# Block 0's output rows stored from the GpSimd queue behind batch 3's loads instead of from SyncE

## The chip, the cores and the metric

The kernel runs on one core of one Trainium2 chip. The metric is the device time of one execution in microseconds (us), the median over runs. A core has five engines that each work through a queue of their own in order: TensorE (PE, matrix products; PEld are its weight loads), VectorE (DVE), ScalarE (ACT), GpSimd (POOL) and SyncE (SP). They wait for each other through semaphores, and DMA queues move data between DRAM and the on-chip memory.

## What is computed

Eight batches of eight heads with 576 tokens of 64 values go through a linear attention with a norm per head, and the result, seen as 4608 tokens of 512 values, through a bilinear feed-forward layer of width 1536:

```python
def _attn_ref(q, k, v, g_norm):
    kv = np.einsum('bhsd,bhse->bhde', k, v)
    out = np.einsum('bhsd,bhde->bhse', q, kv)
    rms = np.sqrt(np.mean(out * out, axis=-1, keepdims=True) + 1e-06)
    return (out / rms * g_norm).astype(np.float32)

def _moe_ref(x, w_a, w_b, w_out):          # x: 4608 x 512
    a = x @ w_a
    b = x @ w_b
    return (a * b @ w_out).astype(np.float32)
```

Inputs and output are float32; inside, bfloat16 and float16 are used.

## The kernel before

The tokens are cut into nine blocks of 512. Block 0 is computed in the plain way: `std_block` forms a and b, and `o_std` (lines 951 to 986) multiplies by the output weights for four tiles of 128 tokens (L964), copies each result out of its accumulator bank into the buffer `o_sb` (ACT, L980), and stores it to DRAM (line 985, through `store`, line 920; the DMA itself is L932). Blocks 1 to 8 use a scheme with seven products in place of eight: `wino_block` (L860 products, L420 copies on ACT, L879 sums on DVE, L914 elementwise product a*b) and `o_block`/`o_unit` for the output product (L1029 products, L1061 copies on ACT, L1067 sums on DVE, L1014 operand sums on DVE). In `wino_block` four products of a unit go through one accumulator bank X, one after the other: p1, p6, p7, p4. Between two of them ACT copies the bank out (e1, e2, e3 into `u`), and after p4 it copies the bank into `c` (c21) and so frees it for the next unit's p1.

Batches 0 and 1 are loaded by pieces at the start. Batches 2 to 7 are loaded one at a time by `load_node` (line 671) from the POOL queue: two DMAs of q into a DRAM scratch `scr` (L682), five of k (L688, L689) and two of v (L694, L698). SP then transposes the scratch into `qT` (L703). Before the next batch's loads stands a one-element copy on POOL (L677, `gate_t`) that waits until the `qT` of the batch before has landed; for batch 7 a second one (L679) waits also for the normed tokens of batch 5. When k and v are there, PE forms kv (L645, 20 matmuls; the last four of them use the data of L698), ACT copies it (L660, L661), and PE multiplies by q (L353). Batches 5 to 7 take another way, `token_tiles`: five token tiles a batch (L560 on PE, L575 on ACT, L579 on DVE, L586 on ACT, L593 on DVE into `xt`), stored to DRAM by SP (L600), read back transposed by SP (four L615 into `xp`), and scaled by ACT (four L621).

The order on each engine is not written out by hand. Each piece of work is a node with an engine, an assumed duration, a due time and its dependencies, and `Plan.order()` (line 104) lists them: at each step it takes the node that can start first on its engine by the assumed times, with the due time to break ties. What a reader of a node's result has to wait in addition stands in `LAT` (line 74) by the producing engine, 0.1 us where an engine is not listed. For kv of a batch the plan assumes that its data is there `kv_us` after the load node (line 708). These numbers decide the order alone; on the chip the semaphores decide the times. In `load_node` the due times come from the batch's window (`at_win`).

DMAs of one kind of queue take eight completion semaphores in turn. A DMA issued from POOL therefore waits until the POOL DMA eight before it has landed.

Of the kernel before, what the change touches and what calls it, by code (L numbers as in the profile page):

```python
# [70 lines left out]


class Plan:
    LAT = {"PE": 0.27, "SP": 2.2, "ACT": 0.2, "DVE": 0.18}
    OWN = {"ACT": 0.12, "DVE": 0.13}

    def __init__(self, t0):
# [12 lines left out]
    @classmethod  # L90
    def after(cls, n, lat=None):
        return n.end + (cls.LAT.get(n.eng, 0.1) if lat is None else lat)

# [44 lines left out]
def kernel(  # L138
# [11 lines left out]
    nc = tc.nc  # L150
# [162 lines left out]
    def xcols(p, t0, n):  # L313
        return xp[p // 2][:, p % 2, t0 % R : t0 % R + n]
# [91 lines left out]
    def mm_us(n, cols):  # L406
        return n * (cols / 2400 + 0.0025)

    def act_us(n, bias=False):
        return (0.155 if bias else 0.06) + n / 1200  # L410
# [260 lines left out]
    def load_node(b, prio, dep, xt=None):  # L671
        ld = {"k": Buf(RK), "v": Buf(RV), "q": Buf(RQT)}
        scr = scr_pool.tile([NP, S, 2, D], BF16, name="scr", tag="scr")

        def issue():
            if dep is not None:
                nc.gpsimd.tensor_copy(gate_t, dep["q"].tile[0:1, 0, 0:1])  # L677
            if xt is not None:
                nc.gpsimd.tensor_copy(gate_t, xcols(NP - 1, (b - 2) * S, 1)[0:1])  # L679
            qv = q[b].rearrange("(p hl) s d -> hl s p d", hl=2)  # L680
            for hl in range(2):
                nc.gpsimd.dma_start(  # L682
                    out=scr[:, :, hl, :].rearrange("p s d -> s p d"), in_=qv[hl]
                )
            kt = ld["k"].tile
            ks = k[b, :, 0:SA, :].rearrange("h (sp c) d -> sp h c d", c=NCH)
            for c in range(NCH):
                nc.gpsimd.dma_start(out=kt[:, c], in_=ks[:, :, c, :])  # L688
            nc.gpsimd.dma_start(out=kt[0:SB, NCH], in_=k[b, :, SA:S, :].rearrange("h sp d -> sp h d"))  # L689
            for n, src in (("v", v),):  # L690
                t = ld[n].tile[:, 0 : H * (NCH + 1) * D].rearrange(
                    "p (h c d) -> p h c d", h=H, d=D
                )
                nc.gpsimd.dma_start(  # L694
                    out=t[:, :, 0:NCH, :],
                    in_=src[b, :, 0:SA, :].rearrange("h (sp c) d -> sp h c d", c=NCH),
                )
                nc.gpsimd.dma_start(  # L698
                    out=t[0:SB, :, NCH, :], in_=src[b, :, SA:S, :].rearrange("h sp d -> sp h d")
                )  # L700

        def transpose():
            nc.sync.dma_start_transpose(  # L703
                out=ld["q"].tile[:].rearrange("p a s -> p (a s)"),
                in_=scr[:].rearrange("a s h d -> (a s) (h d)"),
            )

        issue_us, q_us, ld["kv_us"] = (15.4, 4.3, 13.0) if dep is None else (9.0, 5.0 if b == 3 else 1.8, 16.0 if b == 3 else 13.0)

        ld["n"] = plan.add(  # L710
            "POOL", issue_us, prio, issue, ([(dep["qn"], 8.0)] if dep else []) + ([(xt, TURN)] if xt else []), [ld["k"], ld["v"]]
        )
        ld["qn"] = plan.add(
            "SP", 2.5, prio, transpose, [(ld["n"], q_us)], [ld["q"]]
        )
        return ld
# [203 lines left out]
    def store(g0, o_sb, queue=None, es=slice(0, d_model)):  # L920
        queue = queue or nc.sync
        i = 0
        while i < 128:
            b, j = divmod(g0 + i, S)
            if b < NE:
                c, sp = divmod(j, EP)
                n = min(128 - i, EP - sp)
                r0, st = b * S + EC * sp + c, EC
            else:
                n = min(128 - i, S - j)  # L930
                r0, st = b * S + j, 1
            queue.dma_start(out=out[r0 : r0 + st * (n - 1) + 1 : st, es], in_=o_sb[i : i + n, es])  # L932
            i += n
# [17 lines left out]
    def o_std(ab, muls, win):  # L951
        w0, w1 = win
        ob = Buf(ROS)
        ng, copied = N0 // 128, []
        for g in range(ng):
            pr = w0 + (w1 - w0) * g / ng
            ps = Buf((RO, RY)[g % 2])

            n1 = None
            for f0 in range(0, FC, OP):  # L960

                def mm(g=g, ps=ps, f0=f0):
                    for fc in range(f0, f0 + OP):
                        nc.tensor.matmul(  # L964
                            ps.tile[:],
                            lhsT=ab.tile[:, fc, g * 128 : (g + 1) * 128],
                            rhs=wo_t[:, fc, :],
                            start=(fc == 0),
                            stop=(fc == FC - 1),
                        )  # L970

                n1 = plan.add(
                    "PE", mm_us(OP, d_model), pr + 0.01 * f0, mm,
                    [(wo_n, 5.8 if f0 + OP <= FC // 2 else 10.6), n1] + [muls[fc] for fc in range(f0, f0 + OP)],
                    [ps] if f0 == 0 else [], [ab],
                )
            o_reads.append(n1)
            n2 = plan.add(
                "ACT", act_us(d_model), pr,
                lambda g=g, ps=ps: nc.scalar.copy(ob.tile[:, g], ps.tile[:]),  # L980
                [n1] + copied[-1:], [ob] if g == 0 else [], [ps],
            )
            copied.append(n2)
            plan.add(
                "SP", 0.45, pr + 1, lambda g=g: store(g * 128, ob.tile[:, g]), [n2], (), [ob]
            )

    def o_unit(r0, ab, muls, osum, pr, du, chunks, pieces, m, w, first, second, X, Y, Z, ob, s2, s3, s4, W):
# [164 lines left out]
    for b in range(2, B):  # L1153
        t = b * S / N0
        at_win[b] = (max(53.0, st[int(t) - 1] + (t % 1) * L[int(t) - 1] - 18), st[int(t)] - 22 + (t % 1) * 12)
        if b >= TB:
            at_win[b] = tuple(x - AHEAD for x in at_win[b])
    loads = {2: load_node(2, 22.5, None)}
    wo_n = load_wo(loads[2])
    turned = {}  # L1160
# [13 lines left out]
    for bi in range(1, nb + 1):  # L1174
        o_win = (st[bi] + 1.0, st[bi + 1] - 1.0) if bi < nb else (st[bi] + O_A, st[bi + 1] + O_B)
        if bi == 1:
            o_std(ab, muls, (o_win[0] + 4.0, o_win[1] + 4.0))
            osum = out_sums(st[2] - 10)
        else:
            o_block(bi - 1, ab, muls, osum, o_win, 2, (RO, RY5, RY5) if B5 <= bi < B6 else (RO, RY, RY), 1)  # L1180
        for b in needs[bi]:
            if b > 2:
                loads[b] = load_node(b, at_win[b - 1][0], loads[b - 1], turned.get(b - 2))
            turned[b] = late_batch(b, loads[b], at_win[b])
        ab, muls = wino_block(bi, (st[bi], st[bi + 1]), wsum)
# [40 lines left out]
```

## Time and profile before

| | us |
|---|---|
| median of 3 runs (295.05 to 295.81) | 295.31 |
| the profiled execution | 295.81 |
| its span, first to last instruction | 293.7 |
| DVE, ACT, POOL busy in the span | 241.4, 191.3, 77.7 |
| L860 matmuls, mean of one (x288 each group) | 0.273 |
| L879 sums on DVE, mean of one (x144) | 0.687 |
| L420 copies on ACT, mean of one (x144) | 0.591 |
| stores of `o_sb` from SP, 256, 192, 128, 64 KB: median to landing | 2.7, 5.2, 2.4, 3.9 |
| loads of v, 512 KB, from POOL: median to landing | 10.7 |

The profiled execution is the slowest of the three runs shown. Times within the span are counted from its first instruction. Matmuls are pipelined: one of 256 columns is listed with 0.27 us, but the next one starts 0.109 us later (two rows of two matmuls start 0.22 us apart), so PE's work is counted in starts, not in listed durations. In the same way DVE's sums of 0.69 us start 0.60 apart, and ACT's copies of 0.59 us 0.47 to 0.50 apart.

### The profile page before, as it was taken

The page shows a single profiled execution, that of the slowest core. Times are in us where ns is not written, and L with a number is a line of the kernel's source. Part 1 is how long each engine was busy: PE and PEld are TensorE (multiplying, and loading weights), DVE is VectorE, ACT ScalarE, POOL GpSimd, SP SyncE. Part 2 cuts the span into 40 slices and gives each one's busy share as a digit, 9 for nine tenths or more (in the row PEclk, how much of TensorE's full clock was granted, in tenths as well). Part 3 has the DMA queues.
Part 4 walks back from the last instruction along what each step waited for, and adds up shares of the span by engine and source line. Part 5 has one row for each costly group of instructions (what it writes and reads, how often), then busy time and mean ns, then how long its engine had stood idle before and what let it go on. Part 6 is the DMA issues. An engine that isn't in the chain of part 4 may idle for free.

```text
span 293.7 us, 6760 instructions
## 1 busy us (share of the span) xinstructions
PE 286.7 (98%) x2646; PEld 237.5 (81%) x2648; DVE 241.4 (82%) x443; ACT 191.3 (65%) x395; POOL 77.7 (26%) x96
## 2 busy tenths in 40 slices
PE   6999999999999999999999999999999999999995
PEld 3645558965888888899988998888988888888884
DVE  5454889893987988799989999979989968698964
ACT  3766767866578777867757866686859546665411
POOL 8844830850092390380000910000000000000000
PEclk9999999999999999999999999999999999999999
DMA  8999999699999999699916999440138000300044
GB/s 177 198 198 199 198 159 167 97 169 181 193 132 169 145 168 171 60 135 204 184 29 132 154 163 156 86 164 20 39 80 173 3 0 2 143 2 0 3 143 143
DMA packets 112644, 36.26 MB, mean 123 GB/s; under 512 B 89061, under 2 KB 108517, under 8 KB 112613
## 3 DMA queue, kind: packets, MB, share of 16 engines
q0 software_dynamic: 77552, 18.44, 66.5%
q1 hardware_dynamic: 34448, 16.70, 27.4%
q10 hardware_dynamic: 612, 0.71, 0.8%
q8 instruction: 20, 0.33, 0.5%
q14 instruction: 12, 0.09, 0.1%
HBM read 37.75 MB, written 14.75 MB: 179 GB/s over the span
## 4 chain that ended last, share of the span: by engine, by line
PE 77%; DVE 9%; DMA 5%; issue 2%; POOL 2%; ACT 2%; SPq 1%; DVEq 0%; ACTq 0%; POOLq 0%
PE bk L860 40%; PE bk L1029 21%; PE bk L387 7%; PE bk L964 3%; DVE c L879 3%; DMA wb_t<-in_moe_w_b_dram 3%; PE bk L645 2%; PE bk L353 1%; PE bk L367 1%; SPq L615 1%; DMA xs<-xt 1%; POOL as L242 1%; DVE xt L593 1%; ACT xp L621 1%; DMA xp<-xs 1%
## 5 line engine op out<-in xcount | busy, mean ns | idle before, releaser
L879 DVE TENSOR_TENSOR c<-bk,u 128x512 f16<-128x512 f32 x144 | 96.5, 687 | 19.7 <-PE bk L860 11.8
L420 ACT COPY u<-bk 128x512 f32<-128x512 f32 x144 | 81.5, 591 | 36.4 <-PE bk L860 29.8
L860 PE MATMUL bk<-xp,wa_t 128*128 128x256 f16 x288 | 55.0, 273 | 0.4 <-ACT c L420 0.3
L860 PE MATMUL bk<-xp,wb_t 128*128 128x256 f16 x288 | 55.0, 273 | 0.0
L860 PEld LDWEIGHTS <-wa_t 128*128 128x128 f16 x384 | 37.1, 98 | 6.1 <-issue 0.8
L1029 PEld LDWEIGHTS <-abt 128*128 128x128 f16 x384 | 37.5, 98 | 4.6 <-issue 0.3
L860 PEld LDWEIGHTS <-wb_t 128*128 128x128 f16 x384 | 37.6, 98 | 4.4
L1029 PE MATMUL bk<-wo_t,abt 128*128 128x256 f16 x288 | 37.0, 273 | 0.1
L860 PE MATMUL bk<-T,sb 128*128 128x256 f16 x192 | 36.6, 273 | 0.0
L860 PE MATMUL bk<-T,sa 128*128 128x256 f16 x192 | 36.6, 272 | 0.0
L420 ACT CAST c<-bk 128x512 f16<-128x512 f32 x48 | 28.0, 587 | 12.1 <-PE bk L860 11.5
L914 DVE TENSOR_TENSOR abt<-c 128x1024 f16<-128x1024 f16 x48 | 32.8, 687 | 0.9
L860 PEld LDWEIGHTS <-sa 128*128 128x128 f16 x288 | 27.9, 98 | 3.6
L860 PEld LDWEIGHTS <-sb 128*128 128x128 f16 x288 | 28.2, 98 | 3.3
L1029 PEld LDWEIGHTS <-as 128*128 128x128 f16 x288 | 28.1, 98 | 3.3
L376 DVE SCALAR_TENSOR_TENSOR xp<-bk,g_col,rs 128x288 f16<-128x288 f32 x40 | 20.3, 514 | 11.2 <-ACT rs L371 11.2
L1061 ACT COPY o_sb<-bk 128x512 f32<-128x512 f32 x30 | 17.6, 586 | 17.3 <-PE bk L1029 16.8
L1029 PE MATMUL bk<-so,as 128*128 128x256 f16 x192 | 25.2, 273 | 0.0
L371 ACT ACTIVATE rs<-bk,eps_t 128x288 f32<-128x288 f32 x40 | 20.1, 507 | 6.4 <-PE bk L367 6.2
L688 POOL DMA_DIRECT2D k_t<-in_k_dram x24 | 21.2, 898 | 0.7 <-issue 0.4
L682 POOL DMA_DIRECT2D scr<-in_q_dram x12 | 19.6, 1636 | 2.4 <-issue 1.2
L1067 DVE TENSOR_TENSOR o_sb<-bk,o_sb 128x512 f32<-128x512 f32 (+1 forms) x26 | 16.7, 647 | 3.4 <-PE bk L1029 2.5
(108 smaller groups left out, 427.7 us busy)
## 6 DMA issues: line engine op xcount, KB each, us to landing
out_dram<-o_sb SPq DMA_DIRECT2D x20, 256.0 KB, 2.7
scr<-in_q_dram POOLq DMA_DIRECT2D x12, 288.0 KB, 7.5
k_t<-in_k_dram POOLq DMA_DIRECT2D x24, 128.0 KB, 7.7
v_t<-in_v_dram POOLq DMA_DIRECT2D x6, 512.0 KB, 10.7
out_dram<-o_sb SPq DMA_DIRECT2D x18, 128.0 KB, 2.4
wa_t<-in_moe_w_a_dram POOLq DMA_DIRECT2D x6, 256.0 KB, 10.7
wb_t<-in_moe_w_b_dram POOLq DMA_DIRECT2D x6, 256.0 KB, 10.9
wo_t<-in_moe_w_out_dram POOLq DMA_DIRECT2D x2, 768.0 KB, 9.5
```

The lines of the kernel that those rows point to most:

```text
L371: nc.scalar.activation(rs, self.s_ps[p, h][:, 0:HF], AF.Abs_reciprocal_sqrt, bias=eps_t)
L376: nc.vector.scalar_tensor_tensor(out=xcols(p, self.b * S + h * HF, HF), in0=self.x_ps[p, h][:, 0:HF], scalar=g_col, in1=self.rs[p, h], op0 ...
L387: nc.tensor.matmul(ps[:, 0:n], lhsT=w[:, kc, fc * 128 : (fc + 1) * 128], rhs=xcols(kc, 0, n), start=(kc == 0), stop=(kc == KC - 1),)
L420: ("ACT", act_us(n), lambda: nc.scalar.copy(*args())),
L682: nc.gpsimd.dma_start(out=scr[:, :, hl, :].rearrange("p s d -> s p d"), in_=qv[hl])
L688: nc.gpsimd.dma_start(out=kt[:, c], in_=ks[:, :, c, :])
L860: nc.tensor.matmul(ps.tile[:, i * n : (i + 1) * n], lhsT=lhs(w, sm)[:, kc, :], rhs=rhs()[:, kc, :], start=start and i == 0 and kc == 0, st ...
L879: lambda: nc.vector.tensor_add(cs(fi, h), full(ps), u.tile),
L914: nc.vector.tensor_mul(t, c[:, :, :, 0], c[:, :, :, 1])
L1029: nc.tensor.matmul(ps.tile[:, sub * EH : (sub + 1) * EH], lhsT=lhs(slice(j, j + 1))[:, 0, sub * 128 : (sub + 1) * 128], rhs=rhs[:, j, :], ...
L1061: lambda: nc.scalar.copy(o(fi, h), bank(X, every)), [dep], takes, frees,
L1067: nc.vector.tensor_add(o(fi, h, subs), bank(ps, subs), other)
```

## The change

In `o_std` the four stores of block 0's output (each two DMAs, since the token rows of batches 0 and 1 cross a boundary: 256 KB a tile, 1 MB together) are issued by POOL and not by SP, with an assumed 1.2 us a node in place of 0.45. `LAT` gets an entry of 6.0 us for POOL, which says when the plan may give `o_sb` to the next writer. And `kv_us` of batch 3 goes from 16 to 14.

```diff
-    LAT = {"PE": 0.27, "SP": 2.2, "ACT": 0.2, "DVE": 0.18}
+    LAT = {"PE": 0.27, "SP": 2.2, "ACT": 0.2, "DVE": 0.18, "POOL": 6.0}
...
-        issue_us, q_us, ld["kv_us"] = (15.4, 4.3, 13.0) if dep is None else (9.0, 5.0 if b == 3 else 1.8, 16.0 if b == 3 else 13.0)
+        issue_us, q_us, ld["kv_us"] = (15.4, 4.3, 13.0) if dep is None else (9.0, 5.0 if b == 3 else 1.8, 14.0 if b == 3 else 13.0)
...
             plan.add(
-                "SP", 0.45, pr + 1, lambda g=g: store(g * 128, ob.tile[:, g]), [n2], (), [ob]
+                "POOL", 1.2, pr + 1, lambda g=g: store(g * 128, ob.tile[:, g], nc.gpsimd), [n2], (), [ob]
             )
```

In the program that comes out of it, the eight DMAs stand in POOL's queue after batch 3's last load (L698) and ahead of batch 4's gate (L677); they are gone from SP's queue, where two stood ahead of batch 3's transpose (L703) and six behind it. On PE batch 3's kv (20 matmuls of L645) stands ten matmuls further ahead. From there on the lists of PE, DVE and ACT differ in order, with the same work in them, to near the end of the program.

## The prediction

> **What bounds the kernel now.** I read the page's first part, then PE's timeline for its gaps, then the queues beside each gap.
>
> ```profile
> PE 286.7 (98%) x2646; PEld 237.5 (81%) x2648; DVE 241.4 (82%) x443; ACT 191.3 (65%) x395; POOL 77.7 (26%) x96
> ```
>
> PE is the bound, and stricter than 98% says: counted in starts (0.109 us for a 256-column matmul), it issues without a gap from about 8 us to its end, apart from three places later than the edit. So the change cannot make PE's work shorter; it can remove these three waits or make new ones. The first, in PE's timeline (start, duration):
>
> ```profile
> 80.34 0.38 PE L860 MATMUL bk<-T,wb_t 128*128 128x256 f16 x2
> 80.82 0.92 PE L1029 MATMUL bk<-wo_t,abt 128*128 128x256 f16 x7
> ```
>
> Two matmuls take 0.22, so L1029 was due at 80.56: 0.26 lost, to the DVE sum L879 of 80.08 to 80.77 that frees its bank. The second, ACT's timeline and one row of PE's:
>
> ```profile
> 189.49 0.59 ACT L420 COPY u<-bk 128x512 f32<-128x512 f32 x1 [0.67 <-PE bk L860]
> 189.97 2.13 ACT L621 ACTIVATE xp<-xp,g_col 128x576 f16<-128x576 f16 x3
> 192.61 0.78 ACT L621 ACTIVATE xp<-xp,g_col 128x576 f16<-128x576 f16 x1 [0.51 <-DMA xp<-xs]
> 193.29 0.57 ACT L420 CAST c<-bk 128x512 f16<-128x512 f32 x1
> ...
> 193.91 0.38 PE L860 MATMUL bk<-xp,wa_t 128*128 128x256 f16 x2 [0.29 <-ACT c L420]
> ```
>
> ACT works in order. The four L621 of batch 6 wait for the last transposed piece, which landed at 192.59, and the copy c21 behind them is held with them. PE, due at 193.45 (193.23 plus two matmuls), needs the bank which that copy frees: 0.46 lost. The third wait is 0.27 before 227.08, behind batch 7's L621 in the same manner. Together 0.99.
>
> What sets the 192.59 is in the chain of waits (start, duration, what):
>
> ```profile
> 182.11 3.74 DMA xs<-xt
> ...
> 186.04 1.17 SPq L615
> ...
> 189.86 2.73 DMA xp<-xs
> ```
>
> The last tile's store was issued at 182.11 and took 3.7 to land, where the one issued at 210.07 took 2.0: it queued behind batch 7's qT transpose, which landed at 183.27. Near the edit, POOL's and SP's timelines:
>
> ```profile
> 65.19 0.89 POOL L694 DMA_DIRECT2D v_t<-in_v_dram  x1 [3.12 <-DMA wo_t<-in_moe_w_out_dram]
> 67.43 0.69 POOL L698 DMA_DIRECT2D v_t<-in_v_dram  x1 [1.35 <-DMA scr<-in_q_dram]
> 80.37 0.18 POOL L677 COPY gate_t<-qT 1x1 bf16<-1x1 bf16 x1 [12.25 <-DMA qT<-scr]
> ```
> ```profile
> 67.35 0.79 SPq L932 DMA_DIRECT2D out_dram<-o_sb  x2
> 68.78 6.01 SPq L703 DMA_TRANSPOSE qT<-scr  x1
> 74.89 4.47 SPq L932 DMA_DIRECT2D out_dram<-o_sb  x6
> ```
>
> POOL has nothing to do for 12.25 us. v's two parts took 12.1 and 12.0 to land: 77.2 and 79.4.
>
> **The change, part by part.** Sums are differences, made on the profiled 295.81 (span 293.7, 2.1 around it) and carried to the median 295.31, 0.5 lower.
>
> *SP* loses 0.79 + 4.47 us of issuing. L703 waited for the scratch, not for SP: it started at 68.78, when the scratch landed (68.73). Gain 0.
>
> *POOL* gets eight stores. No store is issued by POOL before; the nearest issues are L698 (0.69) and L694 (0.89), so 8 x 0.69 to 0.89 = 5.5 to 7.1, inside the 12.25. Each also waits for the landing of the POOL DMA eight before. For the first six these are batch 3's scratch and k (68.7 to 73.1), beside their own copies L980 (the last ends at 75.4); for the last two they are v's parts, 77.2 and 79.4. The last store then ends at about 79.4 + 0.3 + 0.7 = 80.4, and the gate, which waits for qT's landing at 80.24, ran at 80.37 anyway: 0. Behind the gate stand batch 4's loads, and behind these in the data queue the stores: 1.05 MB at 336 GB/s (the rate in 79.4 to 82.0, when SP's stores drained) is 3.1, so 82.5 against SP's last landing at 82.2. Batch 4's v landed at 98.7 and PE used it at 102.43, its qT at 99.9 for 104.86. Cover 3.7 and 5.0; cost 0. Without it each microsecond of lateness would be one of PE.
>
> The Trainium skill, "SBUF — State Buffer", section "SBUF: two separate sides", speaks against the move: while DVE runs an operation that takes both shared ports, GpSimd cannot write DMA descriptors. The row to set beside it: from 57.9 to 61.3 DVE was busy for all 3.40 us and four L688 issues took 0.89 each; from 161.1 to 168.5, at 7.07 of 7.40, 0.91. By the rows an issue costs the same beside DVE; by the rule POOL would be held for up to DVE's 9.0 us in 68.2 to 80.3, the stores would end some microseconds later, and batch 4's cover would shrink accordingly.
>
> *Batch 3's loads.* The two early stores (256 KB) leave the stretch before v lands. Unobstructed by them v comes up to 0.26 MB / 207 GB/s (70 to 74 us) = 1.3 earlier, and at least 0 earlier: second part at 78.1 to 79.4. I take 78.8, the middle. qT likewise 79.0 to 80.2.
>
> The skill's "DMA: Bandwidth & Descriptors", "Issuing engines are not separate DMA queues", says that queues share the same engines and that another issuer saves only issue time: by it the gain here would be 0, as the bytes stay; the rows cannot tell, since ahead of the loads and behind them is the same sum.
>
> *kv ten matmuls ahead*: 10 x 0.109 = 1.09, from 79.01 to 77.92. Its last fifth needs v's second part 0.89 later, at 78.81. With 78.8 there is no wait; with 79.43 there is one of 0.62. Range 0 to 0.62, taken 0.2 (the row itself lies at the upper end, the middle at 0). The L353 that needs qT moves to 80.6: after 80.24, 0.
>
> *The wait at 80.82*: L1029 into that bank now stands behind two L353 and six L1029 (0.9), so the DVE sum ends in time: -0.26, or 0 if kv's wait takes its place. Taken -0.2.
>
> *Batch 5's tiles*: its last L593 has one L879 fewer ahead of it on DVE (0.60), but it needs ACT's L586, which ended at 149.77 where L593 ran at 150.09: 0 to -0.3. Its tile's L560 stands 0.44 later on PE. Taken 0. From this hang POOL's gate L679 (160.62, just behind the transposes' landing), batch 7's loads, and so the 183.27 and the 192.59. Batch 6's last L593 gets one L879 more: +0.60 to its store, hidden by the queue (3.7 against 2.0: 1.7 of cover), 0.
>
> So the last landing for batch 6 is 192.59 + 0.2 - 0.2 + 0 = 192.6, between 192.0 (-0.26 - 0.3) and 193.2 (+0.62).
>
> *The order around batch 6's L621.* This decides. In the old list the copy e3 (189.49) of the open unit stands ahead of the four L621, and only its c21 behind. In the new list e3 itself stands behind them, an L1061 ahead. PE's first matmul that needs a held copy is now p4 of that unit, eight matmuls nearer to the start of PE's list: 8 x 0.109 = 0.87. PE resumes at the same 193.9 (last landing + 0.02 + 0.68 + 0.59 + 0.05), but with 0.87 us more work left. The next product but one needs the copy behind it, 0.48 later, and finds 0.44 of work: +0.04. Sum +0.91 with the landing unmoved. A sum on DVE (L1067) before it, 0.44 ahead of PE's reuse of its bank where 0.87 sufficed, costs 0.4 that falls inside the same wait: 0.
>
> *The rest of the new order.* The third wait keeps its place in the lists. New waits are bounded by what the old list shows, 0.99 in 213 us, and below by -0.27, the third wait gone. Nearest is the long stretch from 82 to 193 without one: taken +0.1.
>
> Sum: +0.91 + 0.0 + 0.1 = +1.0: profiled 296.8, median 296.3.
>
> **Rivals.** (1) *The orders converge and nothing shows.* For: the work is the same, the kv of later batches shift by 1.3 us at most, both signs; 0.2 to 0.3 each at 80.8 and batch 5 go as gains into the landing (192.0), which leaves +0.91 - 0.6 = +0.3: 295.6. Against: ACT's list. (2) *Not slower: the transposed pieces come early.* One mechanism: batch 7's qT transpose, 12.3 us here, takes as long as batch 2's 9.9, since the loads beside it started earlier. From 0.9 on the landing makes up for the e3 behind L621; at 2.4 PE would be fed at 191.5 and lose nothing there: -0.46 - 0.26 = -0.7, and with the third wait gone -1.0, 294.3. For: it hangs on DMA timing alone. Against: the spread of the six transposes (9.9 to 12.3) came with their loads, and these have the same bytes. (3) *POOL holds batch 4 up*: stores at the slow 84 GB/s of 82 to 86 us would take 12.5, batch 4's scratch lands some 9 later, less 3.7 of cover: +5, 300. Against: the same stores drained at 336.
>
> **Chances.** A measurement of this kernel tells about 0.3% (0.89 us) from no change. Slower by more, as forecast, 0.50; range of its own 296.2 to 297.5. Rival 1, within, 0.34; rival 2 0.14, all faster; rival 3 0.02. Slower 0.52 together. Low end 294.2: all three waits gone and a little. High end: +0.91 + 0.62 + 0.99 = +2.5, 297.8; I take 297.7. Outside lie half of rival 2, rival 3 and a few hundredths.
>
> **What would show it.** Right: L645 near 77.9; no gap before the L1029 at about 81; in ACT's list L1061, four L621, then a copy to u; PE idle some 1.3 us before an L860 near 193.9 put down to ACT u L420; span 294 to 295.5. Wrong: kv waiting over 0.6 (loads no earlier), the four L621 done before 191.7, or a gap over 0.3 between 82 and 190, which is a wait that I did not see.

## The result, and the profile after

The changed kernel takes 298.61 us (median of 6 runs, 298.21 to 300.36) against 295.23 us of the kernel before (6 runs, 294.99 to 295.81): a ratio of 1.012, with a 95% interval of 1.0094 to 1.0147. It is slower, as forecast, but by 3.4 us where 1.0 was expected, and outside the range. The profiled execution of it took 299.03 us with a span of 297.2, 3.5 us more than the span before.

The page's first part shows the same work, within 1.1 us, on every engine but POOL, which has eight instructions and 4.3 us more, the stores:

```profile
PE 287.5 (97%) x2646; PEld 237.7 (80%) x2648; DVE 241.4 (81%) x443; ACT 192.4 (65%) x395; POOL 82.0 (28%) x104
```

So nearly all of the time went into waits of PE, the engine that was saturated, and into the end of the program behind its last matmuls. PE's timeline around batch 3's kv (start, duration, engine, line, what; in brackets idle time and what ended it):

```profile
78.05 1.06 PE L645 MATMUL bk<-v_t,k_t 128*128 128x128 bf16 x16
79.97 0.38 PE L645 MATMUL bk<-v_t,k_t 128*128 128x128 bf16 x4 [0.86 <-DMA v_t<-in_v_dram]
...
81.50 0.38 PE L860 MATMUL bk<-T,wb_t 128*128 128x256 f16 x2
82.83 0.41 PE L353 MATMUL bk<-qT,kvd 128*128 128x288 bf16 x2 [0.95 <-DMA qT<-scr]
```

Sixteen matmuls of 128 columns (0.056 us each) end at 78.94, so the last four of kv lost 1.03 to v's second part; two of 256 columns end at 81.72, so the L353 lost 1.11 to the transposed q. Neither waited before. The chain of waits now runs through the DMAs in this stretch, where before it ran through PE, DVE and ACT and no DMA:

```profile
56.05 12.51 DMA scr<-in_q_dram
...
68.62 14.17 DMA qT<-scr
82.79 0.04 issue
82.83 0.41 PE bk L353 x2
```

The transpose of batch 3 was issued at the same time as before (68.62 against 68.78) and took 14.2 us to land in place of 11.5. What stood beside it is in POOL's timeline:

```profile
65.08 0.89 POOL L694 DMA_DIRECT2D v_t<-in_v_dram  x1 [3.20 <-DMA wo_t<-in_moe_w_out_dram]
67.27 0.69 POOL L698 DMA_DIRECT2D v_t<-in_v_dram  x1 [1.30 <-DMA scr<-in_q_dram]
69.18 1.07 POOL L932 DMA_DIRECT2D out_dram<-o_sb  x2 [1.23 <-ACT o_sb L980]
70.83 1.09 POOL L932 DMA_DIRECT2D out_dram<-o_sb  x2 [0.57 <-ACT rs L371]
72.48 1.01 POOL L932 DMA_DIRECT2D out_dram<-o_sb  x2 [0.57 <-ACT rs L371]
76.53 0.52 POOL L932 DMA_DIRECT2D out_dram<-o_sb  x1 [3.04 <-ACT u L420]
80.21 0.50 POOL L932 DMA_DIRECT2D out_dram<-o_sb  x1 [3.17 <-DMA v_t<-in_v_dram]
82.92 0.18 POOL L677 COPY gate_t<-qT 1x1 bf16<-1x1 bf16 x1 [2.20 <-DMA qT<-scr]
```

Six of the eight stores (768 KB) are issued by 73.5, and the other two at 76.5 and 80.2, so the whole 1 MB while the transpose is still on its way. Before, SP was busy issuing the transpose until 74.79, and six of the stores came behind it in the same queue. What the queues moved shows the exchange. The transpose's packets (the pieces in which a DMA moves its bytes) are under 512 bytes, those of the stores 2 to 8 KB. Before, from 74.9 to 79.5 us, while SP issued these six stores:

```profile
DMA packets 2517, 0.65 MB, mean 142 GB/s; under 512 B 2260, under 2 KB 2516, under 8 KB 2516
```

After, from 79 to 83 us (then queue, packets, MB, share; q1 is SP's queue, q0 POOL's):

```profile
DMA packets 1157, 0.70 MB, mean 175 GB/s; under 512 B 1046, under 2 KB 1046, under 8 KB 1157
q1 hardware_dynamic: 983, 0.24, 53.6%
q0 software_dynamic: 174, 0.45, 41.6%
```

Before, not one packet of 2 to 8 KB moved in this stretch: the stores waited in SP's queue behind the transpose. After, the transpose's small packets (0.24 MB in 983) shared the DMA engines with 0.45 MB of stores in 111 packets of 2 to 8 KB.

The other places, by PE's starts as in the prediction:

| place | before | after | difference |
|---|---|---|---|
| start of the first L964 (nothing is changed ahead of it) | 60.73 | 60.87 | +0.14 |
| wait in kv for v | 0 | 1.03 | +1.03 |
| wait before L353 for qT | 0 | 1.11 | +1.11 |
| wait before the L1029 at 80.8 for DVE | 0.26 | 0 | -0.26 |
| waits at batch 6's L621 (193 to 196) | 0.46 | 0.92 | +0.46 |
| wait at batch 7's L621 | 0.27 | 0.21 | -0.06 |
| from the last twelve L1029 to the span's end | 5.05 | 6.16 | +1.11 |
| sum; the spans differ by 3.5 | | | +3.53 |

At batch 6 ACT's timeline shows the order that the prediction expected, and then PE's its effect:

```profile
191.76 0.59 ACT L1061 COPY o_sb<-bk 128x512 f32<-128x512 f32 x1 [0.45 <-PE bk L1029]
192.24 2.77 ACT L621 ACTIVATE xp<-xp,g_col 128x576 f16<-128x576 f16 x4
194.91 1.06 ACT L420 COPY u<-bk 128x512 f32<-128x512 f32 x2
```
```profile
193.96 0.38 PE L860 MATMUL bk<-xp,wb_t 128*128 128x256 f16 x2
194.69 0.38 PE L860 MATMUL bk<-xp,wa_t 128*128 128x256 f16 x2 [0.34 <-DVE o_sb L1067]
194.90 0.38 PE L860 MATMUL bk<-xp,wb_t 128*128 128x256 f16 x2
195.53 0.38 PE L860 MATMUL bk<-T,wa_t 128*128 128x256 f16 x2 [0.25 <-ACT u L420]
```

The four L621 run as one block of 2.77 us; no idle time stands inside it. The last transposed piece landed at 192.89, so PE was not held by a landing: it lost 0.51 to a sum L1067 and 0.41 to the copy behind the block.

At the end DVE's chain to the last stores starts later against PE's end. Before and after, DVE's row of L1113 and PE's last group:

```profile
288.00 0.69 DVE L1113 TENSOR_TENSOR o_sb<-o_sb,u 128x512 f32<-128x512 f32 x1
288.65 1.47 PE L1029 MATMUL bk<-wo_t,as 128*128 128x256 f16 x12
```
```profile
290.83 0.69 DVE L1113 TENSOR_TENSOR o_sb<-o_sb,u 128x512 f32<-128x512 f32 x1
291.04 1.47 PE L1029 MATMUL bk<-wo_t,as 128*128 128x256 f16 x12
```

L1113 stands 0.65 ahead of PE's last group before, 0.21 after. Four matmuls (0.44) that stood behind the product it needs now stand ahead of it, so most of the last stores are issued 0.4 later against that group. The very last is not: it is issued 2.00 us after the group's start before and 2.07 after. Nearly all of the 1.11 is in its landing, 2.9 us where it took 1.8 before. The six profiles of the new list have this later order, and there the last landing takes 2.2 to 2.9 us; that the stores, now closer together, wait for each other is likely, but not shown.

### The profile page after: what moved, and what is told of

Read it like the earlier page. It is cut to its first block, busy times and chain, and to the rows that moved or that the text cites. A ratio compares the mean times of both kernels' runs of the same rounds, so it can differ in the third digit from the quotient of the medians.

```text
span 297.2 us, 6781 instructions
## 1 busy us (share of the span) xinstructions
PE 287.5 (97%) x2646; PEld 237.7 (80%) x2648; DVE 241.4 (81%) x443; ACT 192.4 (65%) x395; POOL 82.0 (28%) x104
## 4 chain that ended last, share of the span: by engine, by line
PE 68%; DMA 22%; POOL 4%; ACT 1%; DVE 1%; issue 1%; DVEq 0%; ACTq 0%; SPq 0%; POOLq 0%
PE bk L860 41%; PE bk L1029 23%; DMA qT<-scr 8%; DMA scr<-in_q_dram 8%; DMA wb_t<-in_moe_w_b_dram 6%; PE bk L645 2%; POOL as L242 1%; PE bk L560 1%; POOL scr L682 1%; ACT xp L621 1%; PE bk L353 1%; POOL so L242 1%; PE bk L367 1%; POOL wo_t L725 1%; POOL wa_t L301 1%
## 5 line engine op out<-in xcount | busy, mean ns | idle before, releaser
L879 DVE TENSOR_TENSOR c<-bk,u 128x512 f16<-128x512 f32 x144 | 96.6, 687 | 20.6 <-PE bk L860 16.6
L860 PE MATMUL bk<-xp,wa_t 128*128 128x256 f16 x288 | 55.0, 273 | 0.4 <-DVE o_sb L1067 0.3
L860 PE MATMUL bk<-xp,wb_t 128*128 128x256 f16 x288 | 55.0, 273 | 0.0
L860 PEld LDWEIGHTS <-wa_t 128*128 128x128 f16 x384 | 37.2, 98 | 6.5 <-issue 1.2
L860 PEld LDWEIGHTS <-wb_t 128*128 128x128 f16 x384 | 37.6, 98 | 4.4
L1029 PEld LDWEIGHTS <-abt 128*128 128x128 f16 x384 | 37.5, 98 | 4.4
L1029 PE MATMUL bk<-wo_t,abt 128*128 128x256 f16 x288 | 37.7, 273 | 0.0
L860 PE MATMUL bk<-T,sb 128*128 128x256 f16 x192 | 36.7, 273 | 0.0
L860 PE MATMUL bk<-T,sa 128*128 128x256 f16 x192 | 36.7, 273 | 0.0
L860 PEld LDWEIGHTS <-sa 128*128 128x128 f16 x288 | 27.9, 98 | 3.7
L860 PEld LDWEIGHTS <-sb 128*128 128x128 f16 x288 | 28.2, 98 | 3.3
L1029 PEld LDWEIGHTS <-as 128*128 128x128 f16 x288 | 28.0, 98 | 3.3
L1029 PE MATMUL bk<-so,as 128*128 128x256 f16 x192 | 25.5, 273 | 0.0
L1067 DVE TENSOR_TENSOR o_sb<-bk,o_sb 128x512 f32<-128x512 f32 (+1 forms) x26 | 16.5, 645 | 3.9 <-PE bk L1029 3.8
```

The source lines that it names most:

```text
L860: nc.tensor.matmul(ps.tile[:, i * n : (i + 1) * n], lhsT=lhs(w, sm)[:, kc, :], rhs=rhs()[:, kc, :], start=start and i == 0 and kc == 0, st ...
L879: lambda: nc.vector.tensor_add(cs(fi, h), full(ps), u.tile),
L1029: nc.tensor.matmul(ps.tile[:, sub * EH : (sub + 1) * EH], lhsT=lhs(slice(j, j + 1))[:, 0, sub * 128 : (sub + 1) * 128], rhs=rhs[:, j, :], ...
L1067: nc.vector.tensor_add(o(fi, h, subs), bank(ps, subs), other)
```

## The experiments

Ten kernels ran, called e1 to e10; the program's own copies e1 to e3 are called copies here. "List" is the order of PE, DVE and ACT. Both lists are those of the two kernels shown unless a row says otherwise; they can be joined with any queue for the stores, because the plan's node and the engine that issues the DMA are separate in the code. A kernel with the whole change but kv_us at 16 (built, not run) has, row for row, the lists of before: kv_us alone moves them, the entry in LAT nothing.

| run | list | the eight stores | median us | ratio, 95% interval | v's last part, qT: issue to landing | waits in kv, before L353 |
|---|---|---|---|---|---|---|
| before | before | SP | 295.2 | | 12.0, 11.5 | 0, 0 |
| after | after | POOL | 298.61 | 1.012, 1.0094 to 1.0147 | 12.7, 14.2 | 1.03, 1.11 |
| e1 | after | SP | 296.62 | 1.005, 1.0038 to 1.0062 | 11.8, 11.3 | 0.63, 0 |
| e2 | before | POOL | 295.32 | 1.0008, 0.9998 to 1.0017 | 12.1, 13.9 | 0, 0.19 |
| e3 | after | none | 296.17 | 1.0035, 1.0023 to 1.0047 | 9.9, 11.2 | 0, 0 |
| e4 | after | ACT | 305.33 | 1.0363, 1.0325 to 1.04 | 13.0, 12.6 | see below |
| e5 | after | half POOL, half SP | 296.98 | 1.0063, 1.0051 to 1.0075 | 12.1, 12.7 | 0.67, 0.23 |
| e6 | before | POOL, behind batch 4's loads | 295.18 | 1.0008, 1.0 to 1.0017 | 9.9, 11.2 | 0, 0 |
| e7 | after, one copy moved | POOL | 298.72 | 1.0128, 1.0103 to 1.0153 | 11.4, 14.1 | 0, 2.28 |
| e8 | before, two pairs exchanged | SP | 295.52 | 1.0013, 1.0005 to 1.0022 | 12.1, 11.6 | 0, 0 |
| e9 | before, one pair exchanged | SP | 294.81 | 0.9993, 0.9975 to 1.001 | 12.2, 11.8 | 0, 0 |
| e10 | as e9 | as e6 | 295.04 | 0.9997, 0.9981 to 1.0013 | 10.0, 11.2 | 0, 0 |

**The two halves of the change apart (e1, e2).** e1 is the kernel after with the stores on SP:

```diff
-                "POOL", 1.2, pr + 1, lambda g=g: store(g * 128, ob.tile[:, g], nc.gpsimd), [n2], (), [ob]
+                "POOL", 1.2, pr + 1, lambda g=g: store(g * 128, ob.tile[:, g]), [n2], (), [ob]
```

> The plan, and with it the lists of PE, DVE and ACT, of the kernel after, with the eight stores of block 0 issued by SP again (two ahead of batch 3's transpose, six behind it, as before). Theory A (the six stores on POOL's queue pushed batch 3's transpose back; the lists cost what the prediction said): v's last part lands near 79.4 and qT near 80.2 as before; kv, which needs the last of v at 78.9, waits 0.5; the L353 behind it waits 0; the wait before the L860 near 193 to 195 stays, in all about 1.0 to 1.4 of PE time against before, so 296.2 to 296.6 (1.1 more if the late landing of the last stores, seen after, comes from the lists). Theory B (the new lists are the cause, the queue is not): waits of 1.0 and 1.1 at kv and L353 as after, 298.6.

e2 is the kernel before with the stores on POOL:

```diff
-                "SP", 0.45, pr + 1, lambda g=g: store(g * 128, ob.tile[:, g]), [n2], (), [ob]
+                "SP", 0.45, pr + 1, lambda g=g: store(g * 128, ob.tile[:, g], nc.gpsimd), [n2], (), [ob]
```

> The plan and the lists of PE, DVE and ACT of the kernel before, with the eight stores issued by POOL behind batch 3's loads. Theory A: qT lands near 82.8 instead of 80.2, because the transpose lands only when POOL's queue is empty, and the first L353, due at 82.1 before, waits about 0.7; v's last part near 79.9, just in time for kv in this list (79.9); behind that the old waits, so 0.4 to 0.9 above before: 295.6 to 296.1 (1.1 more if the late landing of the last stores comes from POOL's queue). Theory B: qT as before, 295.2.

The list alone costs 1.5 us, the queue alone 0.2, which its interval does not tell from nothing, and both together 3.4. So the halves are not a sum; 1.7 to 1.8 us come only when they meet. e1's PE timeline has one wait here, 0.63 for v, whose first part landed at 78.2 in this run, and none for qT:

```profile
76.93 0.82 PE L1029 MATMUL bk<-wo_t,abt 128*128 128x256 f16 x6
78.22 1.28 PE L645 MATMUL bk<-v_t,k_t 128*128 128x128 bf16 x20 [0.47 <-DMA v_t<-in_v_dram]
```

e2's has the old wait for DVE and then 0.19 for qT (twelve matmuls from 80.50 end at 81.81):

```profile
80.01 0.38 PE L860 MATMUL bk<-T,wb_t 128*128 128x256 f16 x2
80.50 1.47 PE L1029 MATMUL bk<-wo_t,abt 128*128 128x256 f16 x12
82.00 0.41 PE L353 MATMUL bk<-qT,kvd 128*128 128x288 bf16 x2
```

The sum behind it: before, qT landed 1.9 us ahead of its L353 (80.24, 82.13). The queue takes 2.4 to 2.7 of this (13.9 and 14.2 against 11.5), the list 1.31, because its L353 stands twelve matmuls further ahead. This time by which data lands ahead of its use is its cover. One alone stays within 1 us of zero on either side; both together leave 1.9 - 2.7 - 1.3 = -2.1, and 1.03 + 1.11 = 2.14 was lost. (e2 ended 0.3 below its range: its L353 waited 0.19 and not 0.7, and its trace has no wait at batch 6, of which more below.) Where kv stands does not matter for this sum: what kv does not wait, the L353 behind it waits (e7: 0 and 2.28).

**No stores (e3), half of them (e5).** Is it the bytes of the stores?

```diff
-                "POOL", 1.2, pr + 1, lambda g=g: store(g * 128, ob.tile[:, g], nc.gpsimd), [n2], (), [ob]
+                "POOL", 1.2, pr + 1, lambda: None, [n2], (), [ob]
```

> The kernel after without the eight stores: the rows of block 0's output are not written; the lists of PE, DVE and ACT are those of after. Theory A: nothing stands between v and the transpose: v lands by 78.6, qT by 79.7, no wait at kv or L353; what is left is the order around batch 6's L621, so 0.6 to 0.9 above before: 295.8 to 296.1. Theory B: waits at kv and L353 stay near 1 each, 298 or more.

```diff
-                ... store(g * 128, ob.tile[:, g], nc.gpsimd), [n2], (), [ob]
+                ... store(g * 128, ob.tile[:, g], nc.gpsimd if g < 2 else nc.sync), [n2], (), [ob]
```

> The kernel after with the stores of tiles 0 and 1 (512 KB) on POOL and those of tiles 2 and 3 on SP, behind batch 3's transpose; all lists of PE, DVE and ACT are those of after. Theory A (the transpose lands when the bytes that POOL had queued by then are through): the transpose, 14.2 us from issue to landing with 768 KB of stores in that queue ahead of it and 11.4 with none, takes 11.4 + 2.8 x 512/768 = 13.2; qT lands near 81.8, so kv and L353 together lose about 1.1 where after lost 2.14, and the time is about 297.5. If the last of v or the first 512 KB alone were the cause, the loss stays 2.1 and the time 298.6.

Both came out as theory A has it, e3 0.1 above its range and e5 0.5 below its number. With 0, 512 KB and 1 MB of stores in POOL's queue, issued while the transpose was under way, it took 11.2, 12.7 and 13.9 to 14.2 us: about 1.4 us more for each 512 KB. (The expectation for e5 counted 768 KB for the whole and left out the last two stores, which were issued before the landing too; that is why its 13.2 was too long.) And v: with no store near it, its last part takes 9.9 us; with SP's two early stores 11.8 to 12.2; with POOL's stores behind it in its own queue 11.4 to 12.7. So the prediction's half-sentence that v gains when SP's early stores go away is right (e3, e6), but the stores behind v take the gain back.

**Stores behind batch 4's loads (e6).** In the list of before; the four store nodes are kept aside in `plan.late`, issue from POOL, and are emitted behind batch 4's load node:

```diff
...
+    for n in plan.late:
+        order.remove(n)
+    at = order.index(loads[4]["n"]) + 1
+    order[at:at] = plan.late
...
```

> The lists of PE, DVE and ACT of the kernel before, with the eight stores issued by POOL behind batch 4's loads and not behind batch 3's. Theory A (what counts is that the stores stand in POOL's queue ahead of a transpose that is in flight): batch 3's transpose takes 11.2 to 11.5 as without stores, batch 4's takes about 2.5 longer than the 10.6 of before and lands near 102.5; the first L353 of batch 4 is at 104.9, so nothing is lost, 295.0 to 295.4. Rival C (bytes anywhere in flight delay what is beside them): the same for batch 3, and batch 4's transpose later by less than 1. Rival D (POOL's issuing itself, not the queue): batch 5's loads start 4 later and kv of batch 5 waits.

Batch 3 is clean (9.9 and 11.2), and now it is batch 4's transpose that takes 14.9 us in place of 10.6. From the DMA view of e6, 86 to 106 us (size, median us to landing):

```profile
v_t<-in_v_dram POOLq DMA_DIRECT2D x1, 64.0 KB, 9.9
qT<-scr SPq DMA_TRANSPOSE x1, 14.9
```

It landed at 102.6, its first L353 runs at 104.4, nothing is lost. The delay goes wherever the stores go, larger here (4.3) than expected (2.5). Rival C's "less than 1" is missed; of rival D the first half is true, batch 5's loads start at 103.2 and not at 101.0, but nothing waits for them.

**Stores on ACT (e4).**

```diff
-                ... store(g * 128, ob.tile[:, g], nc.gpsimd), [n2], (), [ob]
+                ... store(g * 128, ob.tile[:, g], nc.scalar), [n2], (), [ob]
```

> The kernel after with the eight stores issued by ACT, at the same place of the plan, and not by POOL; the lists of PE and DVE are those of after. Theory A (a transpose lands behind what POOL's own queue holds): qT lands by 80.8, since the bytes are on another queue, and the wait at L353 is under 0.2; the total near that of the stores on SP, 296.2 to 296.8. Rival C (any bytes that are in flight beside the transpose push it back, whichever queue holds them): qT near 82.8 and the total near 298.6. ACT's own eight issues cost it some 3 us between 69 and 78, where it is not the bound.

Both were wrong on the total, 305.33, for a reason of another kind. ACT's timeline:

```profile
74.88 0.58 ACT L980 COPY o_sb<-bk 128x512 f32<-128x512 f32 x1 [1.81 <-PE bk L964]
81.00 0.80 ACTq L932 DMA_DIRECT2D out_dram<-o_sb  x2
81.85 1.07 ACT L420 COPY u<-bk 128x512 f32<-128x512 f32 x2 [6.38 <-DMA qT<-scr]
```

The seventh store could not be issued before the transpose had landed (80.93). SP's and ACT's DMAs take eight semaphores in turn, and the one this store needs is the transpose's. ACT works in order, so its copies stood behind that store for 6.4 us, and PE lost 6.05 at 76.4. On the disputed point: six stores on ACT's queue, all landed by 79.4, held the transpose: it took 12.6 us, 1.4 more than with no stores (11.2), where four on POOL's queue (512 KB, e5) cost 1.5. So both readings hold in part: stores on either of the other two queues push it back, those on ACT's less for their bytes. Why is open. Two differences are on record: two of ACT's six were issued ahead of the transpose, and the same 1.05 MB went in 512 packets of 2 to 8 KB on ACT's queue and in 256 on POOL's.

**The order around batch 6's L621 (e7, e8).** e7 is the kernel after with the copy e3 ahead of the block; e8 is the kernel before with c21 ahead of it, and with one sum L879 ahead of a L1014 near 80. Both have the first of these edits, e8 the second too:

```diff
+    scaled = [normed[6, i, 0] for i in range(4)]
+    copy = next(n for n in order[order.index(scaled[3]) + 1 :] if n.eng == "ACT")
+    for n in scaled:
+        order.remove(n)
+    at = order.index(copy) + 1
+    order[at:at] = scaled
...
+    add = next(i for i, n in enumerate(order) if n.eng == "DVE" and 80.1 < n.start < 80.2)
...
+    order[add - 1 : add + 1] = [order[add], order[add - 1]]
```

> The kernel after with one copy (L420, e3 of the open unit) ahead of the four L621 of batch 6 in ACT's list, and nothing else moved. If the 0.41 before the L860 at 195.5 is this copy's place, as the prediction had it, that wait is gone and 298.6 becomes 298.2; the 0.51 two matmuls pairs before, where a bank waits for DVE's sum L1067, stays. If ACT's four L621 of 2.77 us only pass the wait on to the copy behind them, the time stays 298.6.

> The kernel before with two pairs exchanged: the copy c21 (L420) ahead of batch 6's four L621 in ACT's list, and the sum L879 one place ahead of a L1014 in DVE's list near 80. Both waits of PE that these cause in the kernel before (0.26 at 80.6 and 0.46 at 193.5) should go: 0.5 to 0.7 less than before, 294.4 to 294.7. If the waits only move on to the next copy, 295.1.

In e7 the 0.41 is gone from where it was and 0.47 stands two products later; the median did not move, though with runs from 297.7 to 300.1 it could not have told 0.4. In e8 the wait near 80 is gone, but the block of L621 now starts at 191.47, behind a copy that PE releases, and PE waits twice as long as before (194.31 to 195.25):

```profile
190.99 0.58 ACT L420 CAST c<-bk 128x512 f16<-128x512 f32 x1 [0.93 <-PE bk L860]
191.47 2.77 ACT L621 ACTIVATE xp<-xp,g_col 128x576 f16<-128x576 f16 x4
194.15 0.56 ACT L1061 COPY o_sb<-bk 128x512 f32<-128x512 f32 x1
194.61 1.07 ACT L420 COPY u<-bk 128x512 f32<-128x512 f32 x2
```
```profile
194.09 0.38 PE L860 MATMUL bk<-xp,wb_t 128*128 128x256 f16 x2
195.25 0.38 PE L860 MATMUL bk<-T,sa 128*128 128x256 f16 x2 [0.78 <-ACT u L420]
```

So it is not one copy's place: 2.7 us of work on ACT stand in one piece ahead of copies of which PE needs one every half microsecond, and whichever copy comes next is late. In the list of before the wait depends on when the last transposed piece lands: 0.46 where that was 192.59, none in e2, e6, e9 and e10, where the block ran without a stop. The profiled run of before, the slowest of its six, is thus not typical here: a run of the old list without this wait is 0.5 shorter, and against it the new list's place costs 0.92 and not 0.46. In the list of after it is 0.92 (0.91 in e3) in every run but e7's, with the last piece landed at 190.7 (e3) as at 192.9 (after).

**Looking for a version that beats both (e9, e10).** e9 is the kernel before with the exchange in DVE's list alone, e10 adds the stores of e6.

> The kernel before with one exchange alone: the sum L879 one place ahead of a L1014 in DVE's list near 80. The wait of 0.26 before the L1029 at 80.8 is gone, as in the run with both exchanges, and the order around batch 6's L621 is as before: 294.9 against 295.2. If PE's time is only lost again at a later wait, 295.2.

> The same exchange in DVE's list, and the eight stores issued by POOL behind batch 4's loads. If the two do not touch each other, the wait at 80.6 is gone, batch 3's transpose takes 11.2 and batch 4's about 14.9 with no wait behind it: 294.7 to 295.0, the fastest of all by 0.1 to 0.2 at most, which these rounds may not tell from no change.

In both traces the wait near 80 is gone, and only the 0.27 at batch 7 is left of the three waits of before. The times, 294.81 and 295.04 against 295.06, do not tell this from no change. No version here beats the kernel before by what can be measured.

## Why the prediction was wrong

**The step that failed** is in "Batch 3's loads": v's "second part at 78.1 to 79.4" and "qT likewise 79.0 to 80.2". They landed at 79.9 and 82.8. The prediction let the stores drain behind batch 3's loads, found the bytes ahead of the loads and behind them "the same sum", and asked only what the stores would do to batch 4. It did not ask what else was in flight on another queue: the transpose, issued at 68.6 and 14 us on its way. The rows to see it were there: batch 3's qT landed 0.8 us behind POOL's last load (80.24, 79.43), batch 4's 1.2 (99.87, 98.71), batch 5's 1.0, batch 7's 0.5. A transpose that lands each time within about a microsecond of the other queue's end may well follow that queue when it is made longer; e3, e5 and e6 show that it does. From this step came the zero and the 0.2 that were 2.14: no wait for qT "after 80.24, 0", and kv's wait "taken 0.2". The first of the prediction's own signs of failure, kv waiting over 0.6, is what happened.

The skill's rule that was weighed there ("DMA: Bandwidth & Descriptors", "Issuing engines are not separate DMA queues") pointed the right way: another issuer gave no bandwidth. The same page, in "Queues, rings and completion order", says that each DMA engine takes turns between the queues that have work, packet by packet. The rows from 79 to 83 us agree as far as they go: both queues moved bytes at once, and the one with large packets moved about twice as many. By that rule an earlier issue does not protect a transfer from another queue, and putting the stores on POOL was not putting them behind the transpose. How far it is the whole reason is not settled: e4's stores on a third queue weighed less, and whether the page's packet is the profile's packet is not shown.

**SP and POOL**: right. The transpose was issued as soon as the scratch had landed, as before. The eight issues took 0.50 to 0.56 us each, 4.2 together, under the 5.5 to 7.1 estimated from load rows, and the rule on DVE and GpSimd ("SBUF — State Buffer") did not show, with DVE busy for 9.28 of the 11.53 us from the first of them to the last. The last store was issued by 80.7 (predicted 80.4). The gate L677 ran at 82.9 and not at 80.4, held by qT, not by the stores.

**Batch 4's cover**: right. Its v and qT landed at 101.2 and 102.3 and nothing waited.

**The wait at 80.8**: right. Predicted -0.2, measured -0.26.

**Batch 6's L621**: the order was as predicted, but the term was mis-sized; that the whole loss there, 0.92, looks like the predicted +0.91 is luck. The prediction let the last landing release PE, kept the old 0.46 and added 0.91. In every run of this list but e7 the block runs without a stop from where ACT is free, and its own length sets the wait; the old wait is replaced, not added to, so the term is +0.46 against the profiled run of before. The sum L1067, put at 0.4 "inside the same wait", was that: 0.51 of the 0.92.

**The rest of the new order**, "taken +0.1": mis-sized. The end of the program has no term in it. From PE's last twelve L1029 to the end of the span, six profiles of the list of before show 4.99 to 5.05, six of that of after 5.50 to 6.16: the list costs 0.45 to 1.1 there, in the landing of the last store.

**The rivals**: the forecast of the sign was right, but of the 3.5 us between the profiles only 0.46 came from the place that was said to decide. Rival 2's mechanism was there: batch 7's transpose took 11.2 us in place of 12.3, and the last piece landed only 0.3 later than before with PE 2.0 later. It gained nothing, since the block of L621 was no longer waiting for it. Rival 3 named POOL and batch 4, where it was batch 3 and the DMA engines. With the list alone (e1), where the failed step does not enter, the time was 296.62, near the 296.3 forecast for the whole. That is partly luck: in its trace kv waited 0.63 for 0.2 and the end cost 0.7 for a term of 0.1, and batch 6 cost 0.46 for 0.91.

## What to carry to other kernels

Before moving a transfer to another queue, list what is in flight on the other queues from its issue to its landing, and look whether that lands each time at the end of the queue you are about to lengthen. Two edits that each eat a part of one cover must be summed against that cover, not costed apart: here 0.2 and 1.5 us made 3.4. And a number in a plan that moves work ahead by 1 us (kv_us) is only as good as the landing it trusts, which the other half of the same change made later.

## What the runs showed of the hardware that was not expected

A wait of PE can cost more than its length. In e7, which has batch 3's list of after, v came early, so kv did not wait and the whole wait fell before the L353 in one piece of 2.28 us. PE's timeline and then the granted clock in windows (window, PE busy, clock, DMA share, GB/s):

```profile
80.01 0.38 PE L860 MATMUL bk<-T,wb_t 128*128 128x256 f16 x2
82.51 0.64 PE L353 MATMUL bk<-qT,kvd 128*128 128x288 bf16 x2 [2.12 <-DMA qT<-scr]
82.95 1.48 PE L1029 MATMUL bk<-so,as 128*128 128x256 f16 x6
```
```profile
82.00:83.00 1.00, 0.49 (x3) 0.72 0.00 0
83.00:84.00 1.00, 1.00 (x6) 0.50 0.00 0
84.00:85.00 1.00, 1.00 (x7) 0.50 0.00 0
85.00:86.00 1.00, 1.00 (x7) 0.57 0.57 37
86.00:87.00 1.00, 1.00 (x11) 1.00 2.16 138
```

PE came back at half its clock and stayed there for about 3.4 us, at 0.213 us a matmul: some 1.6 us more in PE's starts (from this L353 to the L860 behind the next twelve L1029 and an L367 it took 3.24 us, in the profile of after 1.68). In the profile of after the same loss, split into 1.03 and 1.11, left the clock at 1.00 throughout. After the 6.05 us of e4 the clock was 0.50 until 86. The mean clock of each run agrees: e7's two slowest, 299.97 and 300.1 us, have 0.993 and 0.994, its others 0.996 to 1.000. The slowest of after, 300.36, has 1.000, so its time has another reason. The skill ("TensorE: Matmul & The Clock Gate", "Part 1: The HAM clock gate") has an idle window of about 3.4 us, running free, behind which the clock halves; in this profile a wait of 2.3 us was enough.

A DMA of 64 KB, issued before others on the same queue, was not always safe from them: v's last part took 9.9 us alone and 11.4 to 12.7 with stores issued 1.2 us and more behind it on POOL. That was batch 3; in batch 4, with e6's stores right behind it, the same load took 9.9 us against 9.6 before, so something else has a part in it. And a DMA on ACT can wait for one of SP's: e4's seventh store stood 5.5 us for the semaphore of SP's transpose.
